# A fixed table for the order of TensorE's steps, an on-chip normalisation of the last head pair, and chunk loads by single transfers

## The chip, the cores and the metric

The kernel runs on one core of a Trainium2 chip. The metric is the device time of one execution in microseconds, the median of the runs shown. TensorE is called PE here, VectorE DVE, ScalarE ACT, GpSimd POOL, and SyncE, which issues the DMAs in the order of its queue, SP.

## The reference

One token sequence of 2048 rows and 640 columns passes through a layer norm, and then through an attention block (32 heads of 20 columns) and an S²-MLP mixer block side by side; the input and both results are added.

```python
def _A_ref(x, wqkv, wo):
    qkv = (x @ wqkv).reshape(B, S, 3, H, Dh) ...      # B=1, S=2048, D=640, H=32, Dh=20
    scores = einsum("bhqd,bhkd->bhqk", q, k) * Dh ** -0.5
    o = einsum("bhqk,bhkd->bhqd", softmax(scores), v)
    return o.reshape(B, S, D) @ wo

def _B_ref(x, w1, w2, w3, w4):                        # F = 1536
    h = gelu(layernorm(x) @ w1)
    hs = concat(four column groups of h, shifted by +1, -1, +2, -2 rows) @ w2
    x1 = x + hs
    return x1 + gelu(layernorm(x1) @ w3) @ w4

xn = layernorm(x)
return x + _A_ref(xn, A_wqkv, A_wo) + _B_ref(xn, B_w1, B_w2, B_w3, B_w4)
```

## The kernel before, in words

The program is written down as a list of operations with costs, and a planner (`Plan.schedule`) puts them in order. It keeps a clock for each engine, PE, ACT, DVE, POOL and one for the DMA queue on SP, and always takes the engine that is free first; on it, the ready operation with the smallest key (`pl.key`, a place in attention steps). For PE the generator `products` lists what can start: steps whose operands are ready and for which PSUM slots are free (`SLOTS` = 7 shared tiles of 128x512, at most `MOST` of each kind: 4 for scores, 4 for maxima, 2 for other products, 4 for the output projection). PE works in three modes: `row` (two products on 64 rows of the array each), `col` (four products on 32 columns each) and `full`. The planner adds `SWITCH` (214 ns into row or full mode, 134 ns into col mode) and prefers the present mode by `STAY`. The order that comes out is the order of the instructions in every engine's queue; nothing is reordered afterwards.

Attention works on pairs of heads (16) and halves of the queries (2): 32 blocks (`NB`) of 32 steps (`BU`). For each of the 1024 steps there is

- a maximum step, called `m` below (`max_step`, PSUM tile `pm`): two row-mode matmuls of `kpack` and `zq`, then two DVE reductions into `mx`. It runs `LEAD` = 43 steps ahead of the scores. `max_fin` turns a block's maxima into shifts, transposes them (`pmt`), writes them to `md` and from there into two rows of `zq`;
- a score step, `s` (`unit`, PSUM tile `s`): two row-mode matmuls, then two ACT exponentials into `p` tiles (17 buffers);
- after every second score step a PV step, `p` (PSUM tile `pv`): four col-mode products, which the trace shows as eight matmuls. Column 20 of each head's 32 output rows holds the sum of the exponentials.

Everything else on PE, called `d` (filler), is put between those steps by keys: the q, k and v products (`ps_q`, `ps_k`, `psv`), W1 to W4 of the mixer (all in `ps`), transposes (`tp`, `tz`, `pmt`), and at the end the output projection (`pso`, `psl`). Each operand of such a product is split into a rounded part and the rest, and three part products are summed (`parts`). `twins` runs two such sums at once, one on each half of the array's rows: a first turn, a POOL memset as a fence (`fence`), and a second turn with the halves exchanged.

`block_end` copies a finished block from `pv` to `ob`, writes it to the DRAM tensor `od`, reads the sums back as `sm`, takes reciprocals into `rc` and writes those to `rcd`. After the last W4 step `wo_phase` frees and allocates memory, loads the weights `wos` and the sums so far, `acc` (16 token tiles from `ad`), and then, for each half of the tokens and each of four chunks of 128 head columns, `load_o` fetches `oc` from `od` and `rb` from `rcd`: one transfer for each head that the chunk touches, 20 rows or fewer, for both. It multiplies them, splits the product into two parts (`oT`) and multiplies by `wos` (`pso`). The fifth chunk holds heads 25.6 to 32, the last pair among them; it goes by blocks of 512 tokens through one buffer (`ocl`, `rbl`, `oTl`, PSUM `psl`), and after each the output tiles are written.

Of the kernel before, what the change touches and what calls it, by code (L numbers as in the profile page):

```python
# [21 lines left out]
P = 128  # L22
# [5 lines left out]
QB2 = 2  # L28
# [58 lines left out]
K_OPEN = 0.0  # L87

# [101 lines left out]
class Op:  # L190
    __slots__ = ("eng", "cost", "fn", "deps", "key", "port", "start", "end", "n", "users", "table", "ready", "i", "xfer", "tag", "crit", "alt", "moved", "src", "dyn", "tiles", "mode", "insts", "late")

# [7 lines left out]
class Plan:  # L200
# [23 lines left out]
    def _op(self, eng, cost, fn):  # L224
        o = Op()
        o.eng, o.cost, o.fn, o.deps, o.key, o.port, o.users = eng, cost, fn, [], self.key, False, []
        o.table, o.xfer, o.i = None, 0.0, len(self.ops)
        o.start = o.end = o.crit = None
        o.tag, o.alt, o.moved, o.src = "-", None, False, {}
        o.dyn, o.tiles, o.mode, o.late = (), (), None, 0.0  # L230
        self.ops.append(o)
        return o
# [35 lines left out]

    def group(self, mode, cost, products, dk=0.0, after=None):

# [7 lines left out]
        if after is not None:  # L278
            o.deps.append((after, 1))
        o.mode = mode  # L280
        o.key += dk
# [35 lines left out]
    def schedule(self):  # L317
# [27 lines left out]
        def push(e, o):  # L345
            if e == "pe":
                heapq.heappush(asked[o.dyn[0].kind, o.mode] if need(o) else ready[o.mode], (o.key, o.i, o))
            elif e == o.eng:
                heapq.heappush(avail[e, o.port], (o.key, o.i, o))
            else:  # L350
                heapq.heappush(avail[e, o.alt[3]], (o.key + K_ALT, o.i, o))

        def products():

            t = free["pe"]
            for m in SWITCH:
                for x in MOST:
# [10 lines left out]
        while True:  # L368
# [39 lines left out]
            if e == "pe":  # L408
# [98 lines left out]
def tile_kernel(tc, x, wqkv, wo, w1, w2, w3, w4, out):  # L507
# [25 lines left out]
    pl("pool", 150.0, "memset", onesm, 1.0 / D)  # L533
    scratch = const.tile([1, 1], F32, name="scratch")
    kp = [packs.tile([P, S], F32R, name=f"kpack{i}") for i in range(2)]
    zq = [packs.tile([P, HALF], F32R, name=f"zq{i}") for i in range(3)]
# [3 lines left out]
    def dt(shape, dtype, name):  # L540
        return dram.tile(shape, dtype, name=name)
# [8 lines left out]
    od = dt([NPAIR, 2, P, 512], F32, "od")  # L550
    rcd = dt([H, S], F32, "rcd")
    r2d = dt([NT, P], F32, "r2d")
# [54 lines left out]

    def twins(tiles, sums, n):

        m, last = len(sums[0]), None  # L610
        for turn in range(2):
            after = last and pl.fence(last, scratch)
            for i in range(m):
                step = []
                for h, j in enumerate((turn, 1 - turn)):
                    r = slice(64 * h, 64 * h + 64)
                    lhsT, rhs = sums[j][i]
                    step.append((tiles[j], lhsT[r], rhs[r], dict(start=turn + i == 0, stop=turn == 1 and i == m - 1)))
# [377 lines left out]
    def wo_phase():  # L996
# [3 lines left out]
        sp = pl.pool(name="sop", bufs=2, side="right")  # L1000
        ws = wp.tile([P, 2, ND, D], F32R, name="wos")
        for k in range(ND):
            load_row(ws, "wo", k)
        acc = wp.tile([P, NT, D], F32, name="acc")
        for t in range(NT):
            dma(acc[:, t, :], ad[t * P:(t + 1) * P, :], 327680)

        def load_o(k, c0, n, nm, bufs):

            oc = sp.tile([P, n], F32, tag=f"oc{n}", name="oc" + nm, bufs=bufs)  # L1010
            rb = sp.tile([P, n], F32, tag=f"rb{n}", name="rb" + nm, bufs=2 if n > 512 else 1)
            r = 0
            while r < P:
                h, d = divmod(k * P + r, DH)
                m = min(DH - d, P - r)
                q, e = c0 % HALF // 512, h % 2
                src = od[h // 2, c0 // HALF].rearrange("(e q r) n -> e r q n", e=2, q=2)[e, d:d + m, q:q + n // 512]
                dma(oc[r:r + m, :].rearrange("m (q n) -> m q n", n=512), src, m * n * 4)
                dma(rb[r:r + m, :], rcd[h:h + 1, c0:c0 + n].to_broadcast([m, n]), m * n * 4)
                r += m  # L1020
            for c in range(0, n, 512):
                pl("pool", c_pool(512), "tensor_mul", oc[:, c:c + 512], oc[:, c:c + 512], rb[:, c:c + 512], port=True,
                   alt=("dve", c_dve(512), "tensor_mul", True))
            return oc

        for tb in range(4):
            if tb % 2 == 0:
                ocs = [load_o(k, tb * 512, HALF, f"{k}_{tb}", 4) for k in range(4)]
            oT = [sp.tile([P, 2, 512], F32R, tag="oT", name=f"oT{tb}_{k}", bufs=5) for k in range(4)]
            for k in range(4):  # L1030
                split(oT[k][:, 0], oT[k][:, 1], ocs[k][:, tb % 2 * 512:(tb % 2 + 1) * 512], 512)
            for t in range(tb * 4, tb * 4 + 4):
# [3 lines left out]
                                  range(4)) for n in range(2)], 320)  # L1036
                for n, ps in enumerate(pss):
                    c0, c1 = 320 * n, 320 * (n + 1)
                    pl("dve", c_dve(320), "tensor_add", acc[:, t, c0:c1], ps, acc[:, t, c0:c1], dk=K_FE)
        for tb in range(4):  # L1040
            oT = sp.tile([P, 2, 512], F32R, tag="oT", name=f"oTl{tb}", bufs=5)
            oc = load_o(4, tb * 512, 512, f"l{tb}", 1)
            split(oT[:, 0], oT[:, 1], oc, 512)
            for t in range(tb * 4, tb * 4 + 4):
                j = t % 4 * P
                pss = [pd(f"psl_{t}_{n}", "s")[:, :320] for n in range(2)]
                twins(pss, [parts(lambda p, k: oT[:, p, j:j + P], lambda p, k: ws[:, p, 4, 320 * n:320 * (n + 1)],
                                  range(1)) for n in range(2)], 320)
                for n, ps in enumerate(pss):
                    c0, c1 = 320 * n, 320 * (n + 1)  # L1050
                    pl("dve", c_dve(320), "tensor_add", acc[:, t, c0:c1], ps, acc[:, t, c0:c1], dk=K_FE)
                dma(out[t * P:(t + 1) * P, :], acc[:, t, :], 327680)
        sp.close()
# [73 lines left out]

    def halves(ps, rows, w, w0, x, x0):

        pl.group("row", C_ROW, [  # L1130
            (ps[e], w[64 * e:64 * e + rows, w0:w0 + P], x[64 * e:64 * e + rows, x0:x0 + 512],
             dict(start=True, stop=True)) for e in range(2)])

    def max_step(j):
# [7 lines left out]
        ps = [pd(f"pm{j}_{e}", "m") for e in range(2)]  # L1142
        halves(ps, 60, zq[blk % 3], q8 * P, kp[pair % 2], kb * 512)
        for e in range(2):
            pl("dve", c_dve(512), "tensor_reduce", mx[blk][:, e, q8, kb:kb + 1], ps[e], axis=AX.X, op=ALU.max, dk=K_MX)

    def max_fin(blk):
# [17 lines left out]
        for e in range(2):  # L1165
            adma(_f(zq[blk % 3][64 * e + 60:64 * e + 62, :]), mv[e], 8192)

    def block_end(blk):
# [5 lines left out]
        if blk < NB - 2:  # L1174
            pl.key += REST
        sm = pp.tile([P, n], F32, tag="sm", name=f"sm{blk}", bufs=2)
        src = od[pair, qh].rearrange("(s r) (c n) -> s r c n", r=32, n=n)[:, DH]
        adma(sm, src, 8192, 0.0 if blk >= NB - 2 else LATE)
        rc = pp.tile([P, n], F32, tag="rc", name=f"rc{blk}", bufs=2)
        pl("dve", 185.0, "reciprocal", rc, sm)  # L1180
        dst = rcd[2 * pair:2 * pair + 2, qh * HALF:(qh + 1) * HALF].rearrange("e (c n) -> e c n", n=n)
        adma(dst, rc, 8192)

    def unit(u):
# [4 lines left out]
        pl.key = u + K_S  # L1189
        halves(ps, 62, kp[pair % 2], kt * P, zq[blk % 3], qb * 512)  # L1190
        pl.key = u
# [6 lines left out]
        if kt == KB - 1:  # L1198
            pvs[blk] = ps_v.tile([P, 512], F32, tag="pv", name=f"pv{blk}")
        pl.group("col", KB * C_PV, [(pvs[blk][32 * (2 * e + q):32 * (2 * e + q) + 32, :], vt[pair][:, t, e, :],  # L1200
                         pt[e, q, t % KB], dict(start=t == 0, stop=t == NT - 1, tile_position=(0, 32 * (2 * e + q))))
                        for t in range(kt - KB + 1, kt + 1) for e in range(2) for q in range(QB2)])
        if kt == NT - 1:
# [53 lines left out]
```

## Time and profile before

| | |
|---|---|
| runs | 2022.19, 2023.37, 2023.68 us; median 2023.37 |
| profiled execution | 2022.59 us; span 2020.8 us; mean granted PE clock 0.985 |
| PE busy | 1957.7 us (97%), 17041 matmuls |
| DVE busy | 1588.1 us (79%), of which maxima 1304.6 |
| ACT busy | 1313.3 us (65%), of which exponentials 1098.7 |
| POOL busy | 208.0 us (10%) |
| DMA | 264.47 MB, mean 131 GB/s, one queue |
| idle time before `psl` matmuls | 13.4 us |

In the profile all PE products stand under line 274 and most other operations under line 244, because one helper records them; groups are therefore told apart by the tiles that they write and read. A step of kind `m` or `s` shows as two matmuls, one of kind `p` as eight, a filler product as two. Matmul lengths overlap one another: the distance between starts tells what a step costs, not its length. The busy share counts any time in which some matmul is under way.

### The profile page before, as it was taken

To read this page: it belongs to the slowest core of one execution; us is meant where nothing else is said; L and a number is where in the kernel's file an instruction comes from. 1 tells how busy PE (TensorE), PEld (TensorE's weight loads), DVE (VectorE), ACT (ScalarE), POOL (GpSimd) and SP (SyncE) were. 2 spreads that over 40 slices of the span, in tenths; PEclk is the share of its full clock that TensorE was granted. 3 is DMA by queue.
4 is the path that set the end of the run, shared out by engine and by line. 5 is a ranking of instruction groups with operands and counts; after the bars stand their busy time and mean duration, and the time that the engine had idled before them with its cause. 6 is when DMAs were issued, how large, how long until landed. Compare 5 with 4: busy or idle time off the path is not lost.

```text
span 2020.8 us, 43707 instructions
## 1 busy us (share of the span) xinstructions
PE 1957.7 (97%) x17041; PEld 1228.2 (61%) x17041; DVE 1588.1 (79%) x2787; ACT 1313.3 (65%) x2379; POOL 208.0 (10%) x429
## 2 busy tenths in 40 slices
PE   6899999999999999999999999999999999999996
PEld 4675666555555556565665656564766676664665
DVE  7759888888888887978777987778788788888523
ACT  3254766877767774667776657778576676767370
POOL 3001011100001002200011100000100110000200
PEclk9999999999999999999999999999999999999898
DMA  5564344645544466444436362324523132316513
GB/s 172 168 189 133 108 112 130 184 134 165 143 147 127 133 183 217 132 140 141 148 122 200 109 195 87 109 89 142 135 74 104 55 102 68 89 37 205 134 39 131
DMA packets 231562, 264.47 MB, mean 131 GB/s; under 512 B 59604, under 2 KB 174436, under 8 KB 229556
## 3 DMA queue, kind: packets, MB, share of 16 engines
q1 hardware_dynamic: 231356, 261.69, 43.2%
q8 instruction: 134, 2.20, 0.5%
q14 instruction: 72, 0.59, 0.1%
HBM read 153.15 MB, written 106.50 MB: 128 GB/s over the span
## 4 chain that ended last, share of the span: by engine, by line
PE 83%; DVE 9%; DMA 3%; SPq 2%; issue 1%; ACT 1%; POOL 0%; DVEq 0%; ACTq 0%; POOLq 0%
PE ps L274 24%; PE pv L274 22%; PE s L274 13%; PE pm L274 12%; DVE mx L244 6%; PE ps_k L274 3%; PE ps_q L274 3%; PE psv L274 3%; PE pso L274 2%; SPq L244 2%; DMA od<-ob 1%; PE psl L274 1%; DMA oc<-od 1%; DMA qd<-hl 0%; PE pmt L274 0%
## 5 line engine op out<-in xcount | busy, mean ns | idle before, releaser
L244 DVE TENSOR_REDUCE mx<-pm 128x1 f32<-128x512 f32 x2048 | 1304.6, 683 | 276.4 <-PE pm L274 247.8
L244 ACT ACTIVATE p<-s 128x512 f32<-128x512 f32 x2048 | 1098.7, 600 | 499.1 <-PE s L274 460.3
L274 PE MATMUL pv<-p,v 128*32 128x512 f32 x4096 | 538.0, 609 | 0.2 <-DVE ob L244 0.2
L274 PE MATMUL pm<-kpack,zq 60*128 60x512 f32 x2048 | 466.3, 418 | 9.5 <-DVE mx L244 2.6
L274 PE MATMUL s<-zq,kpack 62*128 62x512 f32 x2048 | 466.3, 426 | 3.6 <-DVE acc L244 1.2
L274 PEld LDWEIGHTS s<-zq,kpack 62*128 62x128 f32 x2048 | 220.3, 186 | 229.1 <-DVE mx L244 97.1
L274 PEld LDWEIGHTS pm<-kpack,zq 60*128 60x128 f32 x2048 | 224.6, 187 | 166.6 <-DVE mx L244 59.8
L274 PE MATMUL ps<-zT,w_w 64*128 64x512 f32 x1440 | 222.2, 393 | 0.4
L274 PEld LDWEIGHTS pv<-p,v 128*32 128x32 f32 x4096 | 92.9, 108 | 183.3 <-issue 174.6
L274 PEld LDWEIGHTS ps<-zT,w_w 64*128 64x128 f32 x1440 | 145.9, 186 | 32.3 <-ACT p L244 4.2
L274 PE MATMUL ps<-zT,gT 64*128 64x320 f32 x1344 | 135.2, 306 | 0.0
L274 PEld LDWEIGHTS ps<-zT,gT 64*128 64x128 f32 x1344 | 119.4, 186 | 4.4
L274 PE MATMUL psv<-wv,xT 64*128 64x320 f32 x960 | 95.9, 315 | 3.3 <-ACT vst L244 2.6
L274 PE MATMUL ps<-w2s,gT 64*128 64x320 f32 x960 | 97.9, 308 | 0.9 <-ACT p L244 0.6
L274 PE MATMUL ps<-xT,w_w 64*128 64x512 f32 x600 | 95.1, 395 | 0.8 <-DVE pre L244 0.6
L262 POOL MEMSET scratch<- 1x1 f32 x134 | 11.9, 89 | 783.9 <-PE ps L274 535.1
L274 PEld LDWEIGHTS ps<-w2s,gT 64*128 64x128 f32 x960 | 84.5, 186 | 9.6 <-ACT p L244 1.7
L274 PEld LDWEIGHTS psv<-wv,xT 64*128 64x128 f32 x960 | 81.5, 190 | 13.9 <-ACT vst L244 3.3
L274 PE MATMUL ps<-w2s,hs 64*128 64x320 f32 x960 | 88.2, 312 | 0.2
L274 PEld LDWEIGHTS ps<-w2s,hs 64*128 64x128 f32 x960 | 76.6, 185 | 18.6 <-issue 5.2
L274 PE MATMUL ps_q<-xT,w_q 64*128 64x512 f32 x480 | 76.0, 396 | 0.4 <-POOL scratch L262 0.2
L274 PE MATMUL ps_k<-xT,w_k 64*128 64x512 f32 x480 | 75.3, 395 | 0.4 <-POOL scratch L262 0.2
(145 smaller groups left out, 1283.7 us busy)
## 6 DMA issues: line engine op xcount, KB each, us to landing
zq<-qd SPq DMA_DIRECT2D x156, 80.0 KB
kpack<-kd SPq DMA_DIRECT2D x78, 160.0 KB
w_w<-wd_w SPq DMA_DIRECT2D x48, 256.0 KB
gd<-pre SPq DMA_DIRECT2D x8, 1536.0 KB
g<-gd SPq DMA_DIRECT2D x64, 192.0 KB
wd_w<-ph_w SPq DMA_DIRECT2D x34, 320.0 KB
vd<-vst SPq DMA_DIRECT2D x32, 256.0 KB
kd<-hl_k SPq DMA_DIRECT2D x16, 512.0 KB
```

The source lines that it names most:

```text
L244: getattr(e, m)(val(out), *[val(x) for x in ins], **{k: val(v) for k, v in kw.items()})
L262: o.insts = [nc.gpsimd.memset(scratch.get(), 0.0)]
L274: o.insts = [nc.tensor.matmul(out.get(), lhsT.get(), rhs.get(), **kw) for out, lhsT, rhs, kw in products]
```

## The change

Four edits go together.

1. `ORDER`, a string of 7042 letters, tells for every PE step which kind comes next: `m`, `s`, `p` or `d`. `products` then offers only the next operation of that kind's list (for `d`, the ready one with the smallest key, as before). Kinds are handed in by `halves` and `group`. The other engines and the DMA queue are planned as before, around that order.
2. The last pair does not pass through DRAM. `block_end` keeps its two `ob` tiles, and `normed` picks the sums out of `ob` by a matmul with `pick` (four columns of the identity), takes reciprocals, spreads them to 32 columns each, transposes them back to the layout of `ob` by matmuls, multiplies and splits. `twins` takes these products as extra steps of its second turn (`more`), with weights `wl`, which hold the last 40 rows of `wo` at 32-row places. The fifth chunk becomes 88 rows long, and goes by halves of 1024 tokens; pairs of token tiles 512 apart share a `twins`.
3. For the other pairs `block_end` copies the rows of both heads from `od` into `onm`, laid out by head column, and the reciprocals from `rcd` into `rce`, spread over a head's 20 rows. Both are transfers from DRAM to DRAM; each block has two of each.
4. `load_o` fetches a chunk by one `oc` transfer and two `rb` transfers. `rb` has three buffers of 512 columns, where it had two of 1024.

The rows of `pv` also change places, so that a query block's two heads are neighbours.

```diff
+ORDER = (
+    "dddddddddddddddddddddddddddddddddddddddddddddddddddddddddddddddddddddddddddddddddddddddddddddddddddddddddddddd"
...
+    "sdmddsddmdddsdmdddsmddsdmddmdddsdddmdddsmppmsmpsmspmmspsmdddsdmdddmdddsddmdddmdddmdddmdddddddmdddmppsmsmspmms"
...
@@ schedule
+        turn = iter(ORDER)
+        now = next(turn)
+        line = {c: [o for o in self.ops if o.eng == "pe" and o.kind == c][::-1] for c in "smp"}
+        come = set()
...
         def push(e, o):
-            if e == "pe":
+            if e == "pe" and o.kind != "d":
+                come.add(o.i)
+            elif e == "pe":
...
         def products():
             t = free["pe"]
+            if now != "d":
+                y = line.get(now)
+                if y and y[-1].i in come:
+                    o = y[-1]
+                    n = need(o)
+                    if not n or (len(slots) >= n and held[o.dyn[0].kind] + n <= MOST[o.dyn[0].kind]):
+                        yield max(t, heapq.nsmallest(n, slots)[-1][0]) if n else t, o.mode, [(o.key, o.i, o)]
+                return
...
-                _, _, o = heapq.heappop(y)
+                o = heapq.heappop(y)[2]
+                if now != "d":
+                    line[now].pop()
+                now = next(turn, None)
...
@@ wo_phase
+        def load_o(k, half):
+            m = P if k < 4 else r0
+            cols = slice(half * HALF, (half + 1) * HALF)
+            oc = sp.tile([P, HALF], F32, tag="oc", name=f"oc{k}_{half}", bufs=4)
+            if m < P:
+                pl("pool", 1200.0, "memset", oc[64:], 0.0, port=True)
+            dma(oc[:m], onm[k * P:k * P + m, cols], m * HALF * 4)
+            for c in range(0, HALF, 512):
+                rb = sp.tile([P, 512], F32, tag="rb", name=f"rb{k}_{half}_{c}", bufs=3)
+                dma(rb[:m], rce[k * P:k * P + m, half * HALF + c:half * HALF + c + 512], m * 2048)
+                pl("pool", c_pool(512), "tensor_mul", oc[:m, c:c + 512], oc[:m, c:c + 512], rb[:m], port=True,
+                   alt=("dve", c_dve(512), "tensor_mul", True))
...
+        for half in range(2):
+            oc = load_o(4, half)
...
+            on = normed(half, sp)
+            for j in range(4):
+                ts = [8 * half + 4 * b + j for b in range(2)]
+                for n in range(2):
...
+                    twins(pss, [parts(lambda p, k: oT[b][:, p, js], lambda p, k: ws[:, p, 4, c], range(1))
+                                for b in (0, 1)], 320, first=1,
+                          more=parts(lambda p, k: on[:, p, js], lambda p, k: wl[:, p, c], range(1)))
...
@@ block_end
+        if pair == NPAIR - 1:
+            last[qh] = ob
+            return
         adma(od[pair, qh], ob, 262144)
...
+            adma(onm[h * DH:(h + 1) * DH, cols].rearrange("r (q n) -> r q n", q=2), src[e, :DH], 81920)
...
+            adma(rce[h * DH:(h + 1) * DH, cols].rearrange("r (q n) -> r q n", q=2),
+                 src[e].unsqueeze(0).to_broadcast([DH, 2, 512]), 81920)
+
+    def normed(qh, pool):
+        ob = last[qh]
+        ps = pd(f"pn{qh}", "m")
+        pl.group("full", 1000.0, [(ps[:, 4 * c:4 * c + 4], ob[:, c * P:(c + 1) * P], pick, dict(start=True, stop=True))
+                                  for c in range(4)])
+        rc = pp.tile([P, 16], F32, tag="rc", name=f"rcl{qh}", bufs=2)
+        pl("dve", 80.0, "tensor_copy", rc, ps[:, :16])
+        pl("dve", 185.0, "reciprocal", rc, rc)
+        rx = pool.tile([P, 512], F32, tag="rb", name=f"rx{qh}", bufs=3)
+        pl("dve", c_dve(512), "tensor_copy", rx.rearrange("p (a b) -> p a b", b=32),
+           rc.unsqueeze(2).to_broadcast([P, 16, 32]))
+        ps = pd(f"pb{qh}", "m")
+        pl.group("full", 1000.0, [(ps[:, c * P:(c + 1) * P], rx[:, c * P:(c + 1) * P], ident, dict(start=True, stop=True))
+                                  for c in range(4)])
+        pl("dve", c_dve(512), "tensor_mul", rx, ps, ob)
+        oT = pool.tile([P, 2, 512], F32R, tag="oT", name=f"oTn{qh}", bufs=5)
+        split(oT[:, 0], oT[:, 1], rx, 512)
+        return oT
```

More of the change, by code (lines that the diff above doesn't have):

```diff
@@ L190 @@
 class Op:
-    __slots__ = ("eng", "cost", "fn", "deps", "key", "port", "start", "end", "n", "users", "table", "ready", "i", "xfer", "tag", "crit", "alt", "moved", "src", "dyn", "tiles", "mode", "insts", "late")
+    __slots__ = ("eng", "cost", "fn", "deps", "key", "port", "start", "end", "n", "users", "table", "ready", "i", "xfer", "tag", "crit", "alt", "moved", "src", "dyn", "tiles", "mode", "insts", "late", "kind")
 LAT = {("pe", "act"): 230.0, ("pe", "dve"): 196.0, ("pe", "pe"): 110.0, ("pe", "pool"): 272.0,
@@ L229, in _op @@
         o.tag, o.alt, o.moved, o.src = "-", None, False, {}
-        o.dyn, o.tiles, o.mode, o.late = (), (), None, 0.0
+        o.dyn, o.tiles, o.mode, o.late, o.kind = (), (), None, 0.0, "d"
         self.ops.append(o)
@@ L267, in fence, with group @@
         return o
-    def group(self, mode, cost, products, dk=0.0, after=None):
+    def group(self, mode, cost, products, dk=0.0, after=None, kind="d"):
         nc = self.tc.nc
@@ L279, in group @@
             o.deps.append((after, 1))
-        o.mode = mode
+        o.mode, o.kind = mode, kind
         o.key += dk
@@ L534, in tile_kernel @@
     scratch = const.tile([1, 1], F32, name="scratch")
+    pick = const.tile([P, 4], F32, name="pick")
+    for i in range(4):
+        pl("pool", 60.0, "tensor_copy", pick[:, i:i + 1], ident[:, 32 * i + DH:32 * i + DH + 1])
     kp = [packs.tile([P, S], F32R, name=f"kpack{i}") for i in range(2)]
@@ L550, in tile_kernel @@
     od = dt([NPAIR, 2, P, 512], F32, "od")
-    rcd = dt([H, S], F32, "rcd")
+    onm = dt([D, S], F32, "onm")
+    rcd = dt([NB, 2 * HALF], F32, "rcd")
+    rce = dt([D, S], F32, "rce")
     r2d = dt([NT, P], F32, "r2d")
@@ L606, in parts, with twins @@
         return [(lhs(a, k), rhs(b, k)) for k in kts for a, b in ((0, 0), (0, 1), (1, 0))]
-    def twins(tiles, sums, n):
-        m, last = len(sums[0]), None
+    def twins(tiles, sums, n, first=0, more=()):
+        last = None
         for turn in range(2):
             after = last and pl.fence(last, scratch)
-            for i in range(m):
+            steps = [[sums[0][i], sums[1][i]] for i in range(len(sums[0]))] + [[x, x] for x in more if turn]
+            for i, pair in enumerate(steps):
                 step = []
-                for h, j in enumerate((turn, 1 - turn)):
+                for h, j in enumerate((0, 1) if turn == first else (1, 0)):
                     r = slice(64 * h, 64 * h + 64)
-                    lhsT, rhs = sums[j][i]
-                    step.append((tiles[j], lhsT[r], rhs[r], dict(start=turn + i == 0, stop=turn == 1 and i == m - 1)))
+                    lhsT, rhs = pair[j]
+                    step.append((tiles[j], lhsT[r], rhs[r],
+                                 dict(start=turn + i == 0, stop=turn == 1 and i == len(steps) - 1)))
                 c = c_pe(n)
@@ L1126, in load_v, with halves @@
                 (b - a) * P * 8 * VC)
-    def halves(ps, rows, w, w0, x, x0):
+    def halves(kind, ps, rows, w, w0, x, x0):
         pl.group("row", C_ROW, [
             (ps[e], w[64 * e:64 * e + rows, w0:w0 + P], x[64 * e:64 * e + rows, x0:x0 + 512],
-             dict(start=True, stop=True)) for e in range(2)])
+             dict(start=True, stop=True)) for e in range(2)], kind=kind)
     def max_step(j):
@@ L1166, in max_fin @@
             adma(_f(zq[blk % 3][64 * e + 60:64 * e + 62, :]), mv[e], 8192)
+    last = {}
     def block_end(blk):
@@ L1182, in block_end @@
-        adma(dst, rc, 8192)
+        adma(rcd[blk].rearrange("(p n) -> p n", n=n), rc, 8192)
+        src = rcd[blk].rearrange("(q e n) -> e q n", e=2, q=2)
+        for e in range(2):
+            h = 2 * pair + e
+            adma(rce[h * DH:(h + 1) * DH, cols].rearrange("r (q n) -> r q n", q=2),
[18 more added lines that the diff above has]
+        return oT
@@ L1189, in unit @@
         pl.key = u + K_S
[L1190 removed]
+        halves("s", ps, 62, kp[pair % 2], kt * P, zq[blk % 3], qb * 512)
         pl.key = u
```

138 lines of the change are left out of this document (98 added, 40 removed).

## The prediction, made before the change was run

> **What bounds the kernel now.** I read the page's busy shares first, then the costliest groups, then the stretches between kernel phases.
>
> ```profile
> span 2020.8 us, 43707 instructions
> PE 1957.7 (97%) x17041; PEld 1228.2 (61%) x17041; DVE 1588.1 (79%) x2787; ACT 1313.3 (65%) x2379; POOL 208.0 (10%) x429
> L244 DVE TENSOR_REDUCE mx<-pm 128x1 f32<-128x512 f32 x2048 | 1304.6, 683 | 276.4 <-PE pm L274 247.8
> L244 ACT ACTIVATE p<-s 128x512 f32<-128x512 f32 x2048 | 1098.7, 600 | 499.1 <-PE s L274 460.3
> ```
>
> PE reads 97% busy, so it looks as if at most 63 us could be won. That share hides something, which the timeline shows. Columns: start, length, engine, tiles, count.
>
> ```profile
> 1830.89 0.50 PE L274 MATMUL s<-zq,kpack 62*128 62x512 f32 x2
> 1831.23 0.40 PE L274 MATMUL pm<-kpack,zq 60*128 60x512 f32 x2
> 1831.57 1.07 PE L274 MATMUL pv<-p,v 128*32 128x512 f32 x8
> 1832.56 0.50 PE L274 MATMUL s<-zq,kpack 62*128 62x512 f32 x2
> 1832.90 0.40 PE L274 MATMUL pm<-kpack,zq 60*128 60x512 f32 x2
> 1833.14 0.40 PE L274 MATMUL s<-zq,kpack 62*128 62x512 f32 x2
> 1833.46 1.07 PE L274 MATMUL pv<-p,v 128*32 128x512 f32 x8
> 1974.88 2.78 PE L274 MATMUL pv<-p,v 128*32 128x512 f32 x24
> 1977.59 3.79 PE L274 MATMUL pso<-wos,oT 64*128 64x320 f32 x48
> 1981.21 0.75 PE L274 MATMUL psl<-wos,oTl 64*128 64x320 f32 x8
> ```
>
> Prices, start to start. A score (`s`) or maximum (`m`) step in the middle of its kind: 1833.14 - 1832.90 = 0.24 us. Three PV (`p`) steps in one stretch: 1977.59 - 1974.88 = 2.71, while a PV step alone takes 1832.56 - 1831.57 = 0.99. Two more steps thus add 1.72, 0.86 each, and leaving a PV stretch costs 0.99 - 0.87 = 0.12. The first row step after it takes 1831.23 - 1830.89 = 0.34, 0.10 over its price (weights not loaded ahead). The last one before a stretch takes 1833.46 - 1833.14 = 0.32, 0.09 over. **So each stretch of PV steps costs about 0.315 us of PE time that is counted busy.** A filler step of 320 columns: (1981.21 - 1977.59) / 24 = 0.15.
>
> The Trainium skill, "Perfetto Trace Analysis", § Identifying the Most-Contended Engine, says that matmul busy share is no good measure of headroom. If the busy share were headroom, the switches would be worth nothing and only the idle time could go; by the page they are open to a gain. The rows just shown agree with the page.
>
> **The change part by part.**
>
> *1. The table.* Its 7042 letters fix which kind of step PE takes next. I counted them against the 6990 steps in the timeline of before; its PV rows run from
>
> ```profile
> 124.49 1.06 PE L274 MATMUL pv<-p,v 128*32 128x512 f32 x8
> ```
>
> to the x24 row above, and make 430 stretches with another step between (512 PV steps). The table has 336 stretches for the same 512. 94 x 0.315 = 29.6 us less switching. Which stages can keep it? Stages cut at the same filler step in both orders:
>
> ```profile
> 79.00:187.00 108.00, 103.31 (x884) 70.09 (x880) 82.57 (x143) 43.34 (x90) 8.61 (x26) 0.97 0.61 175
> 187.00:743.00 556.00, 552.66 (x4588) 324.67 (x4584) 474.19 (x800) 408.35 (x746) 51.45 (x123) 0.99 0.48 140
> 856.00:1058.00 202.00, 201.17 (x1601) 123.52 (x1599) 158.90 (x269) 147.41 (x260) 18.21 (x44) 1.00 0.42 136
> 1186.00:1386.00 200.00, 199.35 (x1594) 122.94 (x1596) 152.12 (x249) 142.51 (x246) 3.43 (x24) 1.00 0.35 104
> 1386.00:1840.00 454.00, 452.53 (x4470) 299.34 (x4468) 370.16 (x598) 314.31 (x556) 39.89 (x61) 1.00 0.33 95
> 1840.00:1871.00 31.00, 30.50 (x192) 12.87 (x193) 28.80 (x49) 25.17 (x50) 1.50 (x2) 1.00 0.75 237
> 1871.00:1897.00 26.00, 21.57 (x110) 10.44 (x108) 14.20 (x23) 10.84 (x21) 6.09 (x9) 0.74 0.62 142
> 1977.50:2020.80 43.30, 25.28 (x268) 22.88 (x264) 18.28 (x41) 2.44 (x4) 2.81 (x18) 0.81 0.42 148
> ```
>
> (Columns: stretch, length, busy PE, PEld, DVE, ACT, POOL, granted clock, DMA share, GB/s.) The second to fifth lose 28, 13, 14 and 18 stretches, 73 together; there DVE is busy 76 to 85% and PE 99%, so PE sets the pace and the time is kept: 73 x 0.315 = **23.0 us**. The other 21 lie at 79-187, 743-856, 1058-1186 and after 1840, where fillers run out and DVE (1304.6 / 1024 = 1.27 us a maximum step) or ACT (1098.7 / 1024 = 1.07 us a score step) is about as long as PE: I take nothing. Bounds: 0, if every freed microsecond becomes a wait, and 29.6. I lean to the upper end, because PE's waits named in before are few:
>
> ```profile
> PE psl L274 <- ACT oTl L244: 13.1, 2, 6.8
> PE pso L274 <- ACT oT L244: 3.1, 1, 3.1
> PE pm L274 <- DVE mx L244: 2.6, 6, 0.7
> ```
>
> Against it: neighbouring pairs `ss` rise from 16 to 56 and `mm` from 22 to 45, which gives ACT and DVE less time in between; in its favour, the PV steps that follow their scores within 2 us of PE work fall from 47 to 16.
>
> *2. Loads of the output projection.* Each chunk of heads came in as 20-row pieces of `oc` and `rb`, two transfers a piece; SP (in-order) issues 72 of them in the window 1854 to 1898, from the first to the last:
>
> ```profile
> 1855.18 0.38 SPq L244 DMA_DIRECT2D oc<-od  x1
> 1897.95 0.31 SPq L244 DMA_DIRECT2D rb<-rcd  x1
> ```
>
> Meanwhile PE starves and its clock falls (0.74 at 1871-1897): a PV step takes twice as long after the gap.
>
> ```profile
> 1878.73 1.44 PE L274 MATMUL pso<-wos,oT 64*128 64x320 f32 x8 [3.06 <-ACT oT L244]
> 1882.06 1.93 PE L274 MATMUL pv<-p,v 128*32 128x512 f32 x8
> ```
>
> After the change 12 transfers bring the same first half (one `oc` and two `rb` for each of four chunks). From the last W4 step (1839.5) the old order takes 31 s, 30 m, 16 p and 18 fillers until the first long filler run at 1895.8, 56.3 us. The table has 35 s, 28 m, 20 p, 5 fillers: PE 63 x 0.24 + 20 x 0.87 + 18 stretches x 0.315 + 0.7 = 38.9, ACT 35 x 1.07 = 37.5, DVE 28 x 1.27 = 35.6. The data: 5.2 MB of `acc` (16 x 328 KB) plus 3.1 MB (four `oc` of 524 KB, four `rb` of 262 KB) at the 237 GB/s of 1840-1871 take 35 us, and multiplication and split some 3 more. I take 44 with some waiting; bounds 39 and 56. The Trainium skill, "DMA: Bandwidth & Descriptors", § Why a DMA increments its semaphore by 16 and not by 1, states that a transfer runs on the largest number of engines up to 16 that divides its slowest dimension: 10 for 20 rows, 16 for 128. By that the loads get faster and the 44 would come nearer 39. No run here shows the engines of one transfer.
>
> *3. The last pair.* Old chain after the last PV step: copy, `od` out, sums in, reciprocal out, spread sums in, and four token blocks through one buffer:
>
> ```profile
> 1977.75 0.59 ACT L244 COPY ob<-pv 128x512 f32<-128x512 f32 x1 [7.54 <-PE pv L274]
> 1982.48 0.25 DVE L244 RECIPROCAL rc<-sm 128x16 f32<-128x16 f32 x1 [1.93 <-DMA sm<-od]
> 1995.94 0.69 DVE L244 TENSOR_TENSOR ocl<-ocl,rbl 128x512 f32<-128x512 f32 x1 [3.62 <-DMA rbl<-rcd]
> 1997.38 5.76 PE L274 MATMUL psl<-wos,oTl 64*128 64x320 f32 x48 [6.35 <-ACT oTl L244]
> 2009.92 6.26 PE L274 MATMUL psl<-wos,oTl 64*128 64x320 f32 x48 [6.77 <-ACT oTl L244]
> ```
>
> It leaves two gaps of PE (6.35 + 6.77 us), and the 24 steps after each run at 5.76 / 24 = 0.24 instead of 0.15. The new chain: copy 0.59, selecting matmuls about 1, copy and reciprocal 0.25 each, spreading 0.69, transposing matmuls about 1.2, multiplication 0.69, split 0.62 + 0.69, ten handovers of 0.2: 8 us (the matmuls an estimate; at twice their price 10). 147 fillers follow the last PV letter; 75 of them at least need nothing of the last block, 75 x 0.15 = 11 us. I cost the chain at nothing because of that cover; without it PE would wait up to 8 us and then run slowly. Added: 48 filler steps and 4 groups, 52 x 0.15 = 7.8 us.
>
> *The stage from 1839.5 on, whole.* Left behind the 44 us: 528 fillers x 0.147 = 77.6, 40 s x 0.24 = 9.6, 21 p x 0.87 = 18.3, 7 stretches = 2.2, fences 3, and 4.9 from the last PE row to the end as before. 44 + 115.6 = 159.6, against 2020.8 - 1839.5 = 181.3: **21.7 us less**, though this stage now holds 5 s and 5 p more and 2 m fewer; these leave the earlier stages, 5 x 0.24 + 5 x 0.87 - 2 x 0.24 = **5.1 us less** there.
>
> *4. Added traffic.* Each of 30 blocks gets four more issues (two into `onm`, two into `rce`), 120 x 0.35 = 42 us of SP over 1800 us. I take nothing, because these are keyed late and no reader is near; what covers it is that SP mostly waits. Behind a waiting copy stand the loads of `kpack`, `zq`, `w_w`. The nearest row for such a wait:
>
> ```profile
> SPq L244 <- DMA od<-ob: 66.7, 24, 7.8
> ```
>
> Bounds: 0 and 30 x 2.8 (66.7 / 24) = 83 us, if none of it were covered. `pick` and the `wl` load run beside other work.
>
> **Sum.** 23.0 + 21.7 + 5.1 = 49.8; 2020.8 - 49.8 = 1971.0 span. The profiled execution reads 1.8 us over its span (2022.59) and 0.8 under the median 2023.37: 1971.0 + 1.8 = 1973 us.
>
> **The rivals.** A: ACT and DVE waits eat the freed switch time (the `ss` pairs speak for it, the short PE wait list against): 1973 + 23 = 1996. B: the new end chain is not covered, PE waits 8 us and runs 24 steps slow (0.09 x 24 = 2): 1973 + 10 = 1983, or 1990 if the projection loads also gain nothing against their 56 us bound (12 less 5 of it moved). C, the other side: SP stands behind DRAM-to-DRAM copies whose source has not landed and W tiles or `kpack` come late. At 2.8 us for each of 30 blocks uncovered it ends at 1973 + 83 = 2056; it turns slower than before from 50 / 30 = 1.7 us a block. Against it: a block lasts some 55 us and loads are asked for a block ahead. D: the table does not bring fewer stretches on the chip and the end gains are offset: 2023.
>
> **How the numbers follow.** Forecast 0.55, A 0.20, B 0.13, C 0.07, D 0.05. The forecast's own range is 1958 to 1988: below, all 29.6 us of switching are kept (6.6 more), the projection starts after 39 instead of 44 (5) and the fences hide (3); above, two thirds of the 23 us are lost. The range of 8 in 10 also takes in a stretch price of 0.34, the largest that the rounded rows allow (94 x 0.025 = 2), so 1956; and A with B's 10 us on top, so 2006; beyond it lie C and D, 0.12, and little else. A change under 0.2% (4 us) can't be told from none: of D, 0.03 counts as that and 0.02 as faster; faster 0.55 + 0.20 + 0.13 + 0.02 = 0.90, slower 0.07.
>
> **What would show it.** PV rows in 336 stretches; stages 187-743 and 1386-1840 about 9 and 6 us shorter beyond moved work; no clock below 0.9 near 1871-1897 of before; no PE gap over 2 us after the last PV row; `oc` on PE's wait list for less than 5 us. Wrong would be: PE `s` and `pm` waits on ACT and DVE adding up to over 15 us, or SP waits on `od` that end in late `w_w`.

## The result, and the profile after

| | before | after |
|---|---|---|
| median of the runs | 2022.78 us | 1938.84 us |
| lowest to highest | 2022.11 to 2023.68 | 1935.54 to 1941.29 |
| profiled execution, its span | 2022.59, 2020.8 | 1941.29, 1939.5 |

The ratio is 0.959, with an interval of 0.9575 to 0.9604. The forecast was 1973 us, the range 1956 to 2006: the sign was right, the size was not. 84 us went where 50 were forecast. Medians here and below are over undisturbed runs: one of the four runs of `light2_split`, of 6249.13 us, is left out. Each ratio is to runs of the kernel before on the same chip beside it; their medians lie between 2020.29 and 2025.36 us.

From the page of the changed kernel, the lines that answer to the first fence of the prediction (the helper's lines are now 343 and 313):

```profile
span 1939.5 us, 43924 instructions
PE 1900.3 (98%) x17169; PEld 1262.4 (65%) x17169; DVE 1578.4 (81%) x2801; ACT 1300.1 (67%) x2368; POOL 233.7 (12%) x443
L313 DVE TENSOR_REDUCE mx<-pm 128x1 f32<-128x512 f32 x2048 | 1296.6, 683 | 246.1 <-PE pm L343 224.1
L313 ACT ACTIVATE p<-s 128x512 f32<-128x512 f32 x2048 | 1091.3, 604 | 472.5 <-PE s L343 441.8
```

PE does more matmuls (17169 for 17041) in 57 us less busy time, and reads 98% busy instead of 97%. DVE and ACT do the same work at nearly the same price (683 ns in both, 604 for 600).

The stretches, cut at the same filler steps as those of before; the last two rows are parts of the end (stretch, length, busy PE, PEld, DVE, ACT, POOL, granted clock, DMA share, GB/s):

```profile
85.50:177.20 91.70, 88.98 (x844) 68.03 (x842) 71.48 (x123) 43.31 (x88) 8.46 (x25) 1.00 0.67 186
177.20:717.30 540.10, 537.57 (x4606) 335.29 (x4602) 467.99 (x796) 404.26 (x741) 56.09 (x124) 1.00 0.52 149
717.30:826.70 109.40, 107.53 (x968) 68.49 (x968) 96.18 (x197) 67.64 (x134) 20.05 (x30) 0.97 0.61 179
826.70:1020.90 194.20, 194.16 (x1598) 127.81 (x1599) 156.41 (x267) 142.71 (x254) 15.39 (x41) 1.00 0.45 144
1020.90:1138.60 117.70, 116.74 (x1076) 72.68 (x1072) 110.17 (x222) 82.25 (x154) 22.98 (x36) 1.00 0.64 200
1138.60:1331.60 193.00, 193.00 (x1587) 128.01 (x1588) 153.62 (x256) 139.60 (x243) 4.54 (x25) 1.00 0.42 125
1331.60:1773.30 441.70, 440.89 (x4431) 301.82 (x4428) 363.83 (x599) 304.95 (x546) 59.59 (x67) 1.00 0.34 101
1773.30:1825.10 51.80, 49.74 (x347) 20.75 (x348) 43.46 (x74) 39.14 (x76) 7.57 (x10) 1.00 0.78 255
1905.00:1939.50 34.50, 29.52 (x346) 24.96 (x344) 19.27 (x42) 2.65 (x5) 3.92 (x18) 0.97 0.40 153
```

The prediction, and the expectations below, speak of "the last W4 step" at 1839.5. The row there is the last filler ahead of the output projection, a transpose (`pmt`); the last W4 matmul ends at 1824.45 before and at 1762.23 after:

```profile
1839.50 0.41 PE L274 MATMUL pmt<-ident,T 128*32 128x128 f32 x2
1772.96 0.38 PE L343 MATMUL pmt<-ident,T 128*32 128x128 f32 x2
```

The stages need only the same step in both orders, so I keep this cut and call it the cut at 1840, after its place in before.

I split the change of each length into three: the steps' own work (0.24 for a score or maximum step, 0.87 for a PV step, 0.15 or 0.23 for a filler), PV stretches at 0.315, and the remainder, which is waits of any kind. These are sums of mine over the steps of the two traces; the length is start of stage to start of next.

| stage of before | before | after | change | work | stretches | remainder |
|---|---|---|---|---|---|---|
| start to 79 | 64.1 | 70.9 | +6.9 | +1.9 | 0 | +5.0 |
| 79-187 | 108.1 | 91.7 | -16.4 | -4.7 | -1.6 (5) | -10.2 |
| 187-743 | 556.2 | 540.1 | -16.1 | +1.7 | -8.8 (28) | -9.0 |
| 743-856 | 112.3 | 109.4 | -2.9 | +0.9 | -2.2 (7) | -1.6 |
| 856-1058 | 202.7 | 194.2 | -8.5 | -0.8 | -4.1 (13) | -3.7 |
| 1058-1186 | 127.8 | 117.7 | -10.2 | +0.5 | -1.9 (6) | -8.8 |
| 1186-1386 | 199.8 | 193.0 | -6.8 | -0.2 | -4.4 (14) | -2.1 |
| 1386-1840 | 454.0 | 441.6 | -12.3 | -4.3 | -5.7 (18) | -2.3 |
| 1840 to the end | 181.0 | 166.2 | -14.8 | +12.5 | -0.9 (3) | -26.3 |

Up to the cut at 1840 66.5 us went: 28.7 for 91 stretches, 5.1 for work moved behind it, and **32.7 for waits, which the forecast had left as they were**. Almost none of these stands in the list of PE's own waits: for score and maximum steps that wait for `mx` or `p` it has 4.3 us before and 3.3 after. They stand in the list of the waits of the weight loads (PEld), which the prediction did not show. Before (us in all, times, longest):

```profile
PEld s L274 <- DVE mx L244: 97.1, 135, 1.7
PEld pm L274 <- DVE mx L244: 59.8, 103, 1.0
PEld pm L274 <- ACT p L244: 59.6, 84, 1.0
PEld s L274 <- ACT p L244: 44.2, 62, 1.7
```

After:

```profile
PEld s L343 <- ACT p L313: 61.7, 88, 1.7
PEld s L343 <- DVE mx L313: 52.3, 77, 0.8
PEld pm L343 <- DVE mx L313: 44.3, 75, 1.2
PEld pm L343 <- ACT p L313: 39.4, 68, 1.1
```

The four add up to 260.7 us before and 197.7 after. A score or maximum step needs one of the seven PSUM tiles for each of its halves, and gets it when a DVE reduction (`mx`) or an ACT exponential (`p`) has read it. Part of such a wait lies beside the matmul that still runs, so the sums are larger than what they cost; they tell who is late. Counted by step, how much later than its price the next one starts, the steps from 100 us to some 170 us before the end are some 86 us late before and 53 after; of that the last releaser is DVE `mx` in some 28 and 11 us, ACT `p` in 19 and 9, and nothing that the profile shows in 27 and 21. These sums move by up to 4 us with the rule for who came last.

From the timeline of the changed kernel's end (start, length):

```profile
1908.62 1.16 PE L343 MATMUL pb<-ident,rx 128*128 128x128 f32 x8
1910.78 1.06 PE L343 MATMUL pn<-pick,ob 128*128 128x4 f32 x8
1914.16 1.16 PE L343 MATMUL pb<-ident,rx 128*128 128x128 f32 x8
1923.35 0.62 ACT L313 CAST oTn<-rx 128x512 fp32r<-128x512 f32 x1 [12.19 <-PE psl L343]
1925.39 0.41 PE L343 MATMUL psl<-wl,oTn 64*128 64x320 f32 x2 [0.37 <-POOL scratch L331]
```

The new chain is there and covered: no gap of PE above 0.4 us in it.

### The profile page after: what moved, and what is told of

Read it like the earlier page. It is cut to its first block, busy times and chain, and to the rows that moved or that the text cites. A ratio compares the mean times of both kernels' runs of the same rounds, so it can differ in the third digit from the quotient of the medians.

```text
span 1939.5 us, 43924 instructions
## 1 busy us (share of the span) xinstructions
PE 1900.3 (98%) x17169; PEld 1262.4 (65%) x17169; DVE 1578.4 (81%) x2801; ACT 1300.1 (67%) x2368; POOL 233.7 (12%) x443
## 4 chain that ended last, share of the span: by engine, by line
PE 87%; DVE 5%; DMA 5%; SPq 2%; ACT 1%; issue 1%; POOL 0%; DVEq 0%; ACTq 0%; POOLq 0%
PE ps L343 24%; PE pv L343 23%; PE s L343 14%; PE pm L343 13%; PE psv L343 3%; PE ps_k L343 3%; DVE mx L313 3%; PE pso L343 2%; PE ps_q L343 2%; SPq L313 2%; PE psl L343 1%; DMA od<-ob 1%; DMA rb<-rce 1%; DMA xr<-in_A_x_dram 1%; DMA qd<-hl 1%
## 5 line engine op out<-in xcount | busy, mean ns | idle before, releaser
L343 PE MATMUL pv<-p,v 128*32 128x512 f32 x4096 | 511.1, 601 | 0.0
L343 PE MATMUL pm<-kpack,zq 60*128 60x512 f32 x2048 | 457.0, 415 | 8.1 <-DVE hl L313 2.6
L343 PE MATMUL s<-zq,kpack 62*128 62x512 f32 x2048 | 452.3, 418 | 2.7 <-DVE x L313 1.5
L343 PEld LDWEIGHTS pm<-kpack,zq 60*128 60x128 f32 x2048 | 231.5, 186 | 132.6 <-DVE mx L313 44.3
L343 PEld LDWEIGHTS pv<-p,v 128*32 128x32 f32 x4096 | 101.6, 109 | 207.2 <-issue 194.4
L343 PE MATMUL psv<-wv,xT 64*128 64x320 f32 x960 | 101.8, 318 | 1.1 <-POOL scratch L331 0.8
L331 POOL MEMSET scratch<- 1x1 f32 x134 | 11.8, 88 | 718.2 <-PE ps L343 447.4
L343 PE MATMUL ps<-w2s,hs 64*128 64x320 f32 x960 | 97.4, 311 | 0.1
L343 PEld LDWEIGHTS psv<-wv,xT 64*128 64x128 f32 x960 | 86.8, 191 | 10.2 <-POOL scratch L331 3.4
L343 PEld LDWEIGHTS ps<-w2s,hs 64*128 64x128 f32 x960 | 84.2, 186 | 12.5 <-issue 3.7
```

Source lines behind the costliest of these rows:

```text
L331: o.insts = [nc.gpsimd.memset(scratch.get(), 0.0)]
L343: o.insts = [nc.tensor.matmul(out.get(), lhsT.get(), rhs.get(), **kw) for out, lhsT, rhs, kw in products]
```

## The experiments

**1. The two halves of the change.** `table_only` is the kernel before with the first 6442 letters of `ORDER`, and its own step-by-step choice behind them. `rest_only` is the kernel after with a table that holds the order of before up to the same filler, and then the same step-by-step choice. These tables end with the first filler of the output projection, some way behind the cut at 1840: it starts at 1871.08 in before and at 1813.94 in the changed kernel. Both kernels have these lines behind the table (here as an edit of the kernel after):

```diff
-                now = next(turn, None)
+                if now is not None:
+                    now = next(turn, None)
+                    if now is None:       # the choice by keys goes on from here
+                        for q in line.values(): ...
```

> The kernel before with the table's letters up to the last W4 step; from there the order is chosen step by step, and the projection loads and the last pair stay as they were. Both theories: the stages up to the last W4 step end at about 1773 us as in the changed kernel (66 us earlier than before), the end stage takes its old 181, so about 1957. If the copies into onm and rce had a share in the 66 us, the time is above 1965.

> The changed kernel with the letters of the kernel before (414 PV stretches up to the last W4 step, 428 in all), and a step-by-step choice from there. Both theories: the last W4 step falls at about 1840 us as before, and the end stage keeps most of its 15 us gain, so about 2005 (2000 to 2012). A time near 2023 would say that the end code brings nothing without its part of the table.

Measured: `table_only` 1960.58 us (ratio 0.9686, 0.9665 to 0.9708), `rest_only` 2019.88 (0.9985, 0.9969 to 1.0002). The table alone is worth 62 us, far over what part 1 allowed it at most (29.6, and 5.1 of moved work). The other parts alone are worth 3 us or nothing: I had expected more of them. The two do not add up to the 84: on top of the new order the other parts bring some 20 us (`table_greedy_end` in experiment 5, 1940.96). In the profiles they shorten the stage behind the cut from 186.2 (`table_only`) to 169.2 us in the new order, and from 181.0 (before) to 172.0 in the old. That execution of `rest_only` loses 6 of these 9 us earlier, 2.2 before 79 and 3.8 in 743-856; two executions of the changed kernel differ by as much there (3.9 and 4.0). In `rest_only` every stage from 856 to 1840 takes its old length to 0.1 us, so the added copies from DRAM to DRAM cost nothing there (rival C), and its weight loads wait as before:

```profile
PEld s L337 <- DVE mx L307: 96.8, 133, 1.4
PEld pm L337 <- DVE mx L307: 59.3, 105, 1.0
PEld pm L337 <- ACT p L307: 58.9, 80, 1.3
PEld s L337 <- ACT p L307: 41.5, 58, 0.8
```

**2. Which half of the table.** Two tables mix the orders: `fill_new_pv_old` has the new order of `s`, `m` and `d` and the PV steps at their old places between the scores (426 stretches); `fill_old_pv_new` the reverse (341 stretches). Beside `rest_only` only the string changes.

> The changed kernel with the new order of score, maximum and filler steps, but the PV steps put in by the old order's places (426 stretches). Theory W (the new order of scores, maxima and fillers takes away waits on ACT and DVE that stand inside PE's busy time, some 33 us; a stretch costs 0.315 us): 33 us under rest_only, about 1972, and about 27 us over the same end with the new PV places. Theory S (the whole gain of the first stages follows the number of PV stretches, 0.68 us each): as rest_only, about 2005.

> The changed kernel with the old order of score, maximum and filler steps and the new places of the PV steps (341 stretches). Theory W: 87 stretches fewer x 0.315 = 27 us under rest_only, about 1978. Theory S: 60 us under it, about 1945. A rival to both, that the two orders only work together (a wait takes the place of each switch when the scores are not moved too): near 2000.

Measured: 2142.86 us (1.0587, 1.0563 to 1.061) and 2139.12 (1.0565, 1.0538 to 1.0592). Both expectations fell, by more than 150 us and in sign. There is no share of the gain that belongs to the PV places and another that belongs to the rest: either half of the new order beside the old other half is 120 us worse than no change, and a table with 341 stretches is as slow as one with 426. So the count of stretches is the smaller part of what an order costs. From the page of `fill_new_pv_old`, and its weight loads' waits:

```profile
span 2141.4 us, 43928 instructions
PE 2073.7 (97%) x17169; PEld 1262.0 (59%) x17169; DVE 1583.2 (74%) x2804; ACT 1307.0 (61%) x2378; POOL 212.8 (10%) x430
```

```profile
PEld s L337 <- DVE mx L307: 83.5, 151, 1.7
PEld s L337 <- ACT p L307: 68.2, 106, 3.8
PEld pm L337 <- DVE mx L307: 66.8, 151, 1.0
PEld pm L337 <- ACT p L307: 48.4, 93, 0.9
```

200 us slower than the changed kernel, PE still reads 97% busy. By the count by step its steps are some 223 us late (77 by DVE `mx`, 59 by ACT `p`), those of `fill_old_pv_new` some 234 (84 and 66). One such step in the timeline of `fill_new_pv_old`:

```profile
751.37 0.19 PEld L337 LDWEIGHTS pm<-kpack,zq 60*128 60x128 f32 x1
751.56 1.29 DVE L307 TENSOR_REDUCE mx<-pm 128x1 f32<-128x512 f32 x2 [1.64 <-PE pm L337]
751.60 0.40 PE L337 MATMUL pm<-kpack,zq 60*128 60x512 f32 x1
752.30 0.18 PEld L337 LDWEIGHTS pm<-kpack,zq 60*128 60x128 f32 x1 [0.75 <-DVE mx L307]
752.31 0.50 PE L337 MATMUL pm<-kpack,zq 60*128 60x512 f32 x1 [0.31 <-DVE mx L307]
```

The first half of the maximum step starts at 751.60, the second only at 752.31, when a reduction has given back a tile. PE's list calls that 0.31 us of idle time; from start to start the half step took 0.71 us where a whole step is priced at 0.24.

**3. Are these waits the length of DVE's and ACT's work?** In `light_*` a maximum reads 128 of its 512 columns; in `light2_*` the exponential does too, and the rest of `p` stays at 1.0 in fixed tiles. The suffixes are the four orders: `before`, `after`, `new_old` (as `fill_new_pv_old`), `old_new`.

```diff
-  ... "tensor_reduce", mx[blk][:, e, q8, kb:kb + 1], ps[e], axis=AX.X, ...
+  ... "tensor_reduce", mx[blk][:, e, q8, kb:kb + 1], ps[e][:, :128], axis=AX.X, ...
   light2 also:
-  ... "activation", pt[e, qb, kt % KB], ps[e], AF.Exp ...
+  ... "activation", pt[e, qb, kt % KB][:, :128], ps[e][:, :128], AF.Exp ...
```

> The kernel before, in its own order of all instructions, with each maximum taken over 128 of the 512 columns (the other scores are left out of the maximum), so a maximum step holds DVE for about 0.4 us instead of 1.27. Theory P (the old order asks for maxima faster than DVE can take them, and PE's weight loads wait for it): it gets 30 to 50 us faster, about 1980. Rival S (the gain is in the number of PV stretches alone): within 10 us of 2022.

> The changed kernel with the same lighter maxima. Theory P: its order already paces the maxima, so it gains less, 10 to 20 us, about 1923, and its lead over the kernel before shrinks from 84 to about 50 to 60 us. Rival S: the lead stays at 84 us.

> The mixed order with new score, maximum and filler steps and old PV places (426 stretches, 2143 us), with the lighter maxima. Theory P: its 200 us over the changed kernel are mostly waits for DVE's maxima, so it falls by over 100 us, to 2000 or less; what then stays over light_after is 90 stretches x 0.315 = 28 us plus PV steps that follow their exponentials too closely. Rival E (PV steps wait for ACT's exponentials, DVE has no part in it): it stays above 2100.

> The mixed order with old score, maximum and filler steps and new PV places (341 stretches, 2139 us), with the lighter maxima. Theory P: falls by over 100 us, to 2010 or less. Rival E: its PV steps leave their exponentials enough time (13 start within 0.45 us of the last one), so by E it should not have been slow at all; it would stay near 2139 if ACT's exponentials held the score steps.

> The order of the kernel before, with maxima over 128 of 512 columns and exponentials over 128 of 512 columns as well (the other columns of the p tiles keep a constant 1), so that both engines that give PSUM tiles back to PE do it early; PE's work is unchanged. Theory P2 (the old order waits for PSUM tiles, and where DVE is made light, ACT is next): now both waits go, 40 to 50 us, to about 1975. Rival S (stretches alone): like light_before, 2000 or more.

> The changed kernel with both lighter. Theory P2: about 20 us faster, near 1918; the lead over light2_before is then what switching (94 stretches x 0.315 = 30 us) and the end (15 to 20 us) are worth, 45 to 60. Rival S: a lead of 79 us as with lighter maxima alone.

> New score, maximum and filler order, old PV places (426 stretches), both lighter. Theory P2: nearly all of its 200 us go; what is left over light2_after is the price of 90 more stretches, 28 us, and some 5 us at the end: about 1950. If the price of a stretch were 0.68 us: 1979. Rival (the mixed orders lose by something else than PSUM tiles): above 2040.

> Old score, maximum and filler order, new PV places (341 stretches), both lighter. Theory P2: within 15 us of light2_after, about 1928, since the stretches are as few. Rival: above 2040.

| order | full work | light | light2 |
|---|---|---|---|
| before | 2022.78 | 2005.6 (0.9911) | 1984.63 (0.9797) |
| after | 1938.84 | 1926.27 (0.952) | 1917.13 (0.9471) |
| new, old PV | 2142.86 | 2080.76 (1.0287) | 2036.71 (1.0065) |
| old, new PV | 2139.12 | 2092.35 (1.0334) | 2028.19 (1.0029) |

Two lines of the page of `light2_before` (the last column is idle time before, and who ended it):

```profile
L311 DVE TENSOR_REDUCE mx<-pm 128x1 f32<-128x128 f32 x2048 | 503.2, 286 | 935.1 <-PE pm L341 928.7
L311 ACT ACTIVATE p<-s 128x128 f32<-128x128 f32 x2048 | 456.5, 276 | 1050.4 <-PE s L341 1004.1
```

With a reduction of 286 instead of 683 ns the gap between the two orders stayed at 79 us of 84, which missed what was expected. In `light_before` the lateness by DVE `mx` fell from some 28 to 5 us, but that by ACT `p` rose from 19 to 33: with one engine quick, the step waits for the other's tile. With both quick the gap falls to 67.5 us, and the two mixed orders are 120 and 111 us over `light2_after` instead of some 200. I had expected 33 and some 11, and of the lighter maxima alone a fall of over 100 us, where these two fell by 62 and 47. Some half of what a mixed order loses beyond its stretches stays (92 of 176 us and 109 of 199), nearer to the rival's figures than to mine. The count by step still has these two some 109 and 127 us late, against 37 in `light2_after`; DVE `mx` and ACT `p` come last in 33 and 51 of it, so a large part is open.

Up to the cut at 1840 the orders of before and after differ by 51.6 us in `light2` (1804.8 and 1753.2) and by 66.5 with full work; less the 33.8 of stretches and moved work, 17.8 against 32.7 us of waits. In the stages from 856 to the cut, which repeat to 0.5 us in two executions of the changed kernel (experiment 5), it is 11.8 against 16.9. So **roughly a third to a half of the waits that went hang on how long DVE and ACT work on a tile**; the rest is left when that work is less than half as long.

**4. The price of a stretch.** `split` is the kernel after with 54 more stretches (390), made by moving a PV step past a neighbour; before the cut at 1840 only. `light2_split` is the same with the light work.

```diff
+ORDER up to the cut at 1840: ppd -> pdp, dpp -> pdp behind a d, ppsd -> pspd, ppmd -> pmpd
```

> The changed kernel with 54 PV stretches more (390), each made by moving one PV step past one neighbouring step. Theory W (a stretch costs 0.315 us; the rest of the gain is waits): 17 us slower plus a few us of waits, 1956 to 1963. Rival S (0.68 us a stretch): 37 us slower, 1976.

> The same 54 stretches more, with the maxima and exponentials over 128 of 512 columns (the other columns of the p tiles stay a constant 1). Theory W: 17 us over light2_after (1917), about 1934. Rival S: 37 us over it, 1954.

Measured: 1959.4 us (0.9673, 0.9659 to 0.9688) and 1937.55 (0.9566, 0.955 to 0.9582), 20.6 and 20.4 over the kernels with 336 stretches, which is 0.38 a stretch in both; by the ratios to the kernel before beside each it is 0.31 and 0.36. By the cut at 1840 it is (1790.7 - 1773.3) / 54 = 0.32 and (1769.8 - 1753.2) / 54 = 0.31. In the stages from 856 to the cut 35 more stretches take 12.4 and 13.0 us, 0.35 and 0.37 each, waits that they cause included. The row of `split` up to the cut:

```profile
14.00:1790.70 1776.70, 1756.30 (x15546) 1145.33 (x15546) 1473.66 (x2591) 1210.09 (x2205) 203.11 (x375) 1.00 0.46 139
```

The forecast's 0.315 lies at the lower edge of that; the price hardly depends on DVE's and ACT's work. At 0.38 the 91 stretches would be 35 us, still not 61.

**5. The end.** `table_greedy_end` is the kernel after with the table ended at the first projection filler, as in experiment 1. `pair_via_dram` is that, with the last pair sent by `od` and `rcd` like the others (no `normed`, no `wl`). `pair_via_dram_late` makes one change more, which holds more projection steps back behind the last PV step, 228 instead of 132; `after_again` is the changed kernel beside it.

```diff
-        if pair == NPAIR - 1:
-            last[qh] = ob
-            return
...
-RATE = {'v': 1.0, 'w1': 1.0, 'x1': 1.0, 'w3': 1.089, 'w4': 0.989, 'wo': 0.921}
+RATE = {'v': 1.0, 'w1': 1.0, 'x1': 1.0, 'w3': 1.089, 'w4': 0.989, 'wo': 0.7}
```

> The changed kernel with the table only up to the last W4 step and a step-by-step choice after it. Theory: the end stage takes what it took with the old letters and the new end code, 171 us against 166 in the changed kernel, so about 1944.

> As table_greedy_end, but the last pair goes through od, onm and rce like the others, and the fifth chunk has all its 128 rows; 52 filler steps and the matmuls of the normalisation are gone (7.8 us of PE). Theory L (the projection loads bring the end's gain, the normalisation on chip the gap-free end): the last 20 us again hold a gap of 8 us or more and slow steps after it, so 2 to 8 us over table_greedy_end, about 1949. Rival N (the larger chunk transfers alone close the gaps, and the normalisation's added steps cost more than they save): 5 us under it, about 1939.

> The kernel with the table up to the last W4 step and the last pair by way of DRAM, in which the last filler's assumed rate goes from 0.921 to 0.7, so that the step-by-step end holds 228 instead of 132 projection matmuls back behind the last PV step. Theory (what is left at the end is one gap of 9.4 us for the last pair's columns, and 96 matmuls behind it that took 10.04 us instead of 7.2 at the rate of full clock): some 96 more fillers at 0.075 us are 7.2 us of cover, the gap falls to about 2 us and the slow matmuls behind it run at full rate, together about 10 us: 1924 to 1928. Rival (the fillers held back leave PE short of work earlier, between the last steps of scores and PV, so that what the gap loses comes back there): 1934 to 1940, with new waits of PE before the last PV step.

> The changed kernel, unaltered, beside the run above: about 1939 under both theories.

Measured: 1940.96 us (0.9574, 0.9558 to 0.9591), 1936.21 (0.9562, 0.9546 to 0.9579), **1927.4 (0.9532, 0.9512 to 0.9553)** and 1934.34 (0.9571, 0.9552 to 0.959). The table behind the first projection filler and the on-chip normalisation move nothing that these intervals tell apart; by theory L the version by DRAM should have been slower. In `pair_via_dram` the wait for DRAM costs a gap and slow matmuls behind it (96 in 10.04 us, where the 96 before the gap took 7.88):

```profile
1900.39 7.88 PE L337 MATMUL psl<-wos,oTl 64*128 64x320 f32 x96
1917.63 10.04 PE L337 MATMUL psl<-wos,oTl 64*128 64x320 f32 x96 [9.37 <-ACT oTl L307]
```

With more steps behind the last PV step both are gone, in `pair_via_dram_late`:

```profile
1889.64 18.17 PE L337 MATMUL pso<-wos,oT 64*128 64x320 f32 x240
1909.94 1.04 PE L337 MATMUL psl<-wos,oTl 64*128 64x320 f32 x12
1911.52 14.43 PE L337 MATMUL psl<-wos,oTl 64*128 64x320 f32 x180 [0.54 <-POOL scratch L325]
```

The time came as expected, 9 us under `pair_via_dram` by the medians, 6 by the ratios: the stage behind the cut at 1840 takes 1931.6 - 1773.9 = 157.7 us, 23.3 less than in before. It is the fastest of all: 7 us under `after_again` on the same chip, though the two intervals touch (0.9553 and 0.9552). The normalisation by DRAM needs 128 matmuls less than the on-chip one (17041 for 17169), and is hidden by work that is there anyway. Whether the on-chip version would also gain from fillers held back was not run.

## Why the prediction was wrong, point by point

**The step that failed is the ceiling of part 1**, "Bounds: 0, if every freed microsecond becomes a wait, and 29.6": it holds only if an order can change nothing but the count of stretches. It put waits for PSUM tiles at nothing, on the ground that "PE's waits named in before are few", read from PE's own list. For score and maximum steps that wait for `mx` or `p` that list has 2.6 us (the row in the prediction) and these:

```profile
PE s L274 <- ACT p L244: 0.9, 3, 0.5
PE pm L274 <- ACT p L244: 0.8, 3, 0.4
```

Together that is 4.3 us; the weight loads' list has 260.7, and 63 of them went, which was worth some 33 us of time. The prediction had itself said of the busy share that it "hides something"; I then used PE's idle list as if it did not. The sign of being wrong that I had named, PE waits of over 15 us, was read from the same list and could not have shown it. By the Trainium skill, "Perfetto Trace Analysis", § Identifying the Most-Contended Engine, matmul busy share is not a good measure of headroom. Here 97 to 98% stands for 1939, 2021 and 2141 us.

**Stages.** The four that I let keep their stretches lost 43.7 us: 23.0 of it stretches, as forecast. The three up to 1186 for which I took nothing lost 29.5, the largest miss: in 79-187 DVE is busy 82.67 of 108.1 us before and 71.48 of 91.7 after, and the steps' own work with its stretches fills some 90 and 84 us of PE, so neither was at its limit; that they waited for each other by turns is how I read it. "ACT or DVE about as long as PE" was true of the steps' prices and said nothing of that.

**Part 2.** The first longer projection run starts at 1818.96 in after, 45.7 us behind the cut at 1840: 44 was forecast. The clock is 1.00 there, as forecast, where before had 0.74. The rule on a transfer's engines would have it nearer 39 (the Trainium skill, "DMA: Bandwidth & Descriptors", § Why a DMA increments its semaphore by 16 and not by 1); no run here tells whether the loads run on more engines. From there to the end it is 120.5 us against 115.6. Most of that is a price that the sum had wrong: it counted the four groups of the normalisation's matmuls as fillers of 0.15 us, 0.6 in all, and from start to start they take 1.97 (`pn`) and 2.18 (`pb`), 4.15 in all. The five stalls of over 0.3 us add up to 3.1, near the 3 put on fences. With 1.7 of the first term that is the end stage's 14.8 instead of 21.7.

**Part 3.** Covered, as argued, and worth nothing: the version by DRAM is as fast, and with more cover it is the fastest, though the intervals touch. The 48 added fillers and the four groups take 7.2 + 4.15 = 11.4 us, where the sum had 7.8; the gap and the slow steps that they replace cost 9.37 + 2.2 = 11.5 in `pair_via_dram`.

**Part 4.** Nothing, as taken: the stages of `rest_only` from 856 to 1840 repeat those of before, and the 6 us lost earlier lie within what two executions differ by.

**Rivals.** None came. A had the freed time turn into waits of ACT and DVE; the waits fell instead. What the prediction lacked is A's mirror image: an order found by looking ahead that also gives tiles back in time.

**What stays open.** The part of the removed waits that does not depend on DVE's and ACT's durations. And no simple count of the letters explains the new order: PE's work between neighbouring maximum steps falls short of DVE's 1.27 us by some 110 us in all in the old order, 130 in the new, 185 and 174 in the mixed ones (at the prices of the table above, up to the cut at 1840). That fits the mixed orders, which wait most; it does not fit that after waits less than before. The PV steps, the longest steps, do not explain it either: they stand between neighbouring maxima in 395 gaps of the old order, in 305 of the new, and in 346 and 292 of the mixed ones. Single executions also differ: in the profile of `after_again` the cut at 1840 falls at 1764.2 instead of 1773.3, so that the 33 us of waits were 42 there.

## What to carry to other kernels

Price an order of steps by start-to-start distances over all steps of a kind, not by the engine's idle list: a two-part step that waits for a buffer between its halves counts as busy, and shows only as a wait of the weight load. When such waits exist, a reordering has no ceiling in switch counts, and halves of a good order cannot be valued one by one. Here a long chain at the end was hidden at least as well by holding independent work back as by rebuilding it.

## What the hardware showed that was not expected

A quarter of the columns does not make a quarter of the time: a maximum takes 286 ns over 128 columns and 683 over 512, an exponential 276 and 600, so about 155 and 170 ns of each are fixed, if the rest grows with the columns (an estimate from two sizes). After 9.37 us without work PE took 10.04 us for 96 matmuls, 2.2 us more than before the gap, so this gap cost about a quarter more than its length. The granted clock accounts for it: it reads 1.00 over 1895 to 1908 us and 0.79 over 1917.6 to 1928, and 7.88 / 0.79 is 9.97.
